# Pooled attention and a two-layer network on one core: transposes by DMA, halved products and new constants in a planner

## The chip, the core and the metric

The kernel runs on one core of one Trainium2 chip. What counts is the device time of one launch in microseconds, the median of a few runs. A core has TensorE (PE, matrix products), VectorE (DVE), ScalarE (ACT, here the exponential and the Gelu), GpSimd (POOL) and SyncE (SP); the last two, and ScalarE once, issue DMAs. TensorE writes its results to PSUM, eight banks of 128 x 512 float32. Each engine works through its own queue in order and waits at an instruction until the semaphores that it names have been raised.

## The reference

Attention with pooled keys, and then a two-layer network on its output:

```python
def _attn_ref(q, kv, w_sr):                  # q (4, 12288, 128), kv (4, 384, 32, 128)
    ...
    kv_pool = kv.reshape(B, H // r, r, W // r, r, C).mean(axis=(2, 4))     # r = 4
    kv_flat = kv_pool.reshape(B, -1, C) @ w_sr                             # 768 keys for each batch
    k = v = kv_flat
    s = scale * (q @ k.transpose(0, 2, 1))
    ...
    return (a @ v)                           # a: the softmax of s

def _moe_ref(x, w_in, w_out):                # x (49152, 128), w_in (128, 2048), w_out (2048, 128)
    h = x @ w_in
    g = h * (1.0 / (1.0 + np.exp(-1.702 * h)))
    return g @ w_out
```

Keys and values are the same numbers, needed in two layouts: keys with the channels on the partitions, values with the key index on the partitions.

## The kernel before

**Tiling.** The 49,152 queries are 96 groups (G = 512). In attention a group has 6 chunks of 128 keys, in the network 16 chunks of 128 hidden units. For every chunk TensorE makes one product of 512 columns into a PSUM bank ("filling": L350 in attention, L596 in the network), ScalarE applies its function to up to three banks in one activation (L352, L598) and writes bf16 to one of 34 frames of three in SBUF, and TensorE multiplies that again ("draining"): in attention 4 products of 129 columns per chunk (L363; the 129th column of the values is one and gives the softmax's sum), in the network one product of 512 columns (L606), accumulated over 16 chunks in one bank. VectorE normalizes the attention output (L386, L389), and turns the network's output bank in blocks of 32 x 32 (L617), from where SP stores it in four DMAs (L619).

**Stages.** Two rounds of 48 groups: attention of groups 0 to 47, their network, attention of 48 to 95, their network. Attention outputs go through DRAM and come back transposed (`put_away`, `bring_back`) as input of the network.

**Banks.** Six of the eight banks are two sets of three which fillings use in turn, so filling p + 2 must wait until activation p has left its set. The other two (four before the activations become three wide) are accumulators, handed out by `acc()`.

**Order.** Everything is placed while the kernel is built, by a planner at the end of the function (L797 to L861). It keeps a model time `now` of TensorE in units of one 512-column product, and `end[p]`, the time at which activation p would end. After each filling it places drains and extras until the next would go past `limit`, the time at which the coming filling must start if its activation is to follow without a gap; then it places that filling. What it has placed stays in that order on the chip, whatever ScalarE really does. The line that says how long an activation is taken to last:

```python
end.append(begin + FIXED + CHUNK * len(part))            # L791; FIXED 0.295, CHUNK 1.978
```

`room_ahead` (free frames) makes it drain when frames run short. At the very end `drain_last` (L622) makes the last group's drains as 64 products of 128 columns in four banks of their own; one of these is the bank of group 94's output ("held"), whose first three products come after the nine of the other banks.

**Offloaded chunks.** A few chunks are computed by VectorE and not by ScalarE: `rolling` and groups 48 to 51 in attention (L415 and `early_exp`), `lent` in the network (L409 and `lent_gelu`). They are 50 of 2112.

**Queries.** Groups 0 to 11 are loaded by POOL's queue with a cast (`load_q`, L222) and transposed on TensorE (`transpose_q`, L236), with a copy by VectorE (L242). From group 12 on POOL casts them to DRAM (`cast_q`, L209) and SP loads them transposed, four groups at a time (`load_qT`, L215), at the groups that TURN names.

**Keys of batches 2 and 3.** They are summed by accumulating DMAs of POOL (`add_kv`, L173), one step for each group of the first network stage from group 2 (batch 2) and 24 (batch 3) on. Then, in two halves a, VectorE adds (`sum_kv`, L179), TensorE transposes the pooled half (L184), and makes keys (`make_k`, L192) and values (`make_v`, L199), each with a copy by VectorE. These three are extras that the planner places between drains.

Of the kernel before, what the change touches and what calls it, by code (L numbers as in the profile page):

```python
# [10 lines left out]
BF = mybir.dt.bfloat16  # L11
# [13 lines left out]
def kernel(  # L25
    ctx, tc, q, kv, w_sr, moe_w_in, moe_w_out, out,
):
    nc = tc.nc
    B, N, C = q.shape
    _, H, W, _ = kv.shape  # L30
    r = 4
# [18 lines left out]
    x_bf = nc.dram_tensor("x_bf", (B * N, C), BF, kind="Internal").ap()  # L50
    q_bf = nc.dram_tensor("q_bf", (B * N, C), BF, kind="Internal").ap()

    kv_r = kv.rearrange("b (ch p) (a w) c -> b a ch p (w c)", p=128, a=2)
# [44 lines left out]
    def acc_bf():  # L98
        return acc().bitcast(BF)
# [20 lines left out]
    def new_keys(b):  # L120
        kTs[b] = kvres.tile([128, J], BF, name="kT")

        vs[b] = kvres.tile([128, JC, C + 8], BF, name="v")
        nc.vector.memset(vs[b][:, :, C:C + 1], 1.0)
# [55 lines left out]

    def transpose_pooled(b, a):
        ps = acc_bf()[:, 0:h].rearrange("p (a b) -> p a b", a=4)
        for wp in range(4):
            nc.tensor.transpose(ps[:, wp, :], pooled[b, a][:, wp, :], ident[:Hp, :Hp])  # L184
        pTs[b, a] = kvtmp.tile([128, h], BF, name="pT")
        nc.vector.tensor_copy(pTs[b, a], ps.rearrange("p a b -> p (a b)"))

    def make_k(b, a):
        ps = acc()
        if a == 0:  # L190
            new_keys(b)
        nc.tensor.matmul(ps[:, :h], w_sr_sb, pTs[b, a], start=True, stop=True)  # L192
        nc.vector.tensor_copy(kTs[b][:, a * h:(a + 1) * h], ps[:, :h])

    def make_v(b, a):
        ps = acc()
        pT = pTs.pop((b, a))
        for k in range(K):
            nc.tensor.matmul(ps[:, k * C:(k + 1) * C], pT[:, k * 128:(k + 1) * 128], w_sr_sb,  # L199
                             start=True, stop=True)  # L200
        nc.vector.tensor_copy(vs[b][:, a * K:(a + 1) * K, 0:C], ps[:, :h].rearrange("p (k c) -> p k c", k=K))
        for jc in range(a * K, a * K + K):
            vs[b, jc] = True
# [13 lines left out]

    QS = 3
    qs = [x_tile(XS - 1 - JC - s) for s in range(QS)]

# [34 lines left out]
    load_q(1, 2, 4)  # L255
    for s in range(2, QS):
        load_q(s, 0, 2)
        load_q(s, 2, 4)
    cast_q(3)
# [70 lines left out]
    early = range(NG // R, NG // R + EARLY)  # L330
    rolling = [(i, JC - 1) for i in [10, *range(38, NG // R, 6), *range(57, 90, 6)]]
    lent = [(g, FCH - 1) for g in range(52, 94) if g % 5 in (2, 4)]
# [189 lines left out]

    TURN = {6: 3, 7: 4, 8: 5, 20: 6, 21: 7, 22: 8, 25: 9, 32: 10, 35: 11, 40: 12}
    CAST = {0: [5], 13: [6], 14: [7], 15: [8], 16: [9], 26: [10, 11], 27: [12]}
# [31 lines left out]
    def background_moe(g):  # L556

        n, g = divmod(g, 4 * XS)
        m, odd = divmod(g - 9, 2)
        m += FIRST  # L560
        if n == 0 and FIRST <= m < RT // PART:
            (bring_back if odd else put_away)(n, m)
        g += n * 4 * XS
        nonlocal low
        if g == 12:
            low = EARLY * JC
            order[:] = [f for f in order if f >= low // K]
        if g in CAST_MOE:
            gate()
            cast_q(CAST_MOE[g])  # L570
        if g in (41, 42):
            load_qT(g - 28)
        if g == 43:
            background(early[0])
        for b, lo in ((2, 2), (3, 24)):
            if lo <= g < lo + 8:
                gate()
                add_kv(b, g - lo)
            if g in (lo + 10, lo + 12):
                use_kv(b, (g - lo - 10) // 2)  # L580

    def use_kv(b, a):
        nonlocal extra_at
        sum_kv(b, a)
        on_dve(3.5)
        extra_at = max(extra_at, dve + 1.5)
        extras.extend([(transpose_pooled, b, a), (make_k, b, a), (make_v, b, a)])

# [10 lines left out]

    def drain_moe(g, fc):  # L600
        if g == NG - 1:
            drain_last(g, fc)
            return
        if fc == 0:
            o_of[g] = acc(("o", g))
        nc.tensor.matmul(o_of[g], w_out_sb[:, fc, :], weights(("m", g, fc)),  # L606
                         start=(fc == 0), stop=(fc == FCH - 1))
        if (g, fc) in lent:
# [102 lines left out]
    def prepare(p):  # L711
# [3 lines left out]
        for i, jc in part:  # L715
# [23 lines left out]
        16: [(key_and_value, 0, 5), (later, 6)],  # L739
        17: [(later, 7)],  # L740
        18: [(later, g) for g in range(8, 12)]}

    FIXED, CHUNK, SWITCH, HANDOVER, EVACUATE = 0.295, 1.978, 6.0, 1.0, 4.5
    COST = {pool_chunk: (1.9, 2.6), key_chunk: (0.3, 2.4), value_chunk: (0.3, 2.4),
            transpose_q: (1.05, 4.2), early_fill: (1.0, 5.5), key_and_value: (0.55, 3.5),
            transpose_pooled: (0.9, 3.6), make_k: (0.8, 3.2), make_v: (0.8, 3.7)}
    COPY = {pool_chunk: 1.5, key_chunk: 1.5, value_chunk: 1.5, key_and_value: 2.8, transpose_q: 3.2}  # L750
# [3 lines left out]
    end, extra_at = [], 0.0  # L754
    source, dve = None, 0.0
    early_left = 2 * (G // T) * EARLY
# [12 lines left out]
    def fill(p):  # L769
# [15 lines left out]
        if p >= 2:  # L785
            now = max(now, end[p - 2] + HANDOVER / 2)
        now += len(part)
        begin = max(now + HANDOVER / 2, end[p - 1] if p else 0.0)
        if p and kind != seq[p - 1][0]:
# [7 lines left out]
    for n in range(len(seq)):  # L797
        fill(n + 2)
        jobs(n + 3)
        while True:  # L800
            room = room_ahead()
            limit = end[-1] - len(seq[n + 3][1]) - HANDOVER if n + 3 < len(seq) else 1e9
            bank = free[next_acc()]
# [10 lines left out]
            if f:  # L814
                now = max(now, bank) + COST[f][0]
                f(*args)
                free[last_acc] = dve + 1.0 if f is early_fill else copied(f)
                if f in (transpose_pooled, make_k, make_v):
                    on_dve(2.5)
                extra_at = max(now + PAUSE, dve + 1.5 if f in (transpose_pooled, make_k, make_v) else 0.0)  # L820
                if f is early_fill:
# [13 lines left out]
            needs = at[("at" if kind == "a" else kind, i, c)]  # L835
            cost = K * SMALL if kind == "a" else 1.0
            halved = kind == "a" and i // TS < SPLIT
            first_of = (c == 0 or halved) and (kind == "m" or i % TS == 0)
            if source is not todo_early and (needs > n or (kind == "a" and first_of and at["at", i + TS - 1, c if halved else 1] > n)
# [5 lines left out]
                break  # L845
            start = now if source is todo_early else max(now, end[needs] + HANDOVER)
            if first_of:
                start = max(start, bank)
            if start + cost > limit and not (room < 2 * K + 1 or (room < 4 * K and start == now)):
                if first_of:  # L850
                    source = None
                break
            now = start + cost
            (drain_attn if kind == "a" else drain_moe)(i, c)
            source.pop(0)
# [37 lines left out]
```

## Time and profile before

| | us |
|---|---|
| runs | 948.50, 948.76, 948.81 (median 948.76) |
| span of the profiled execution | 946.7 |
| Gelu activations of 1536 columns (L598) | 501, 1.496 each as recorded |
| exponentials of 1536 columns (L352) | 161, 1.500 each as recorded |
| first-layer products (L596) | 405.8 busy, 1476 recorded |
| second-layer products (L606) | 402.6 busy, 1477 recorded |
| values' products (L363), 129 columns | 163.0 busy, 2268 recorded |
| query products (L350) | 145.0 busy, 498 recorded |
| query transposes on TensorE (L236) | 4.6 busy, 48 |
| transposes of pooled keys (L184) | 1.3 busy, 16 |
| value products of batches 2 and 3 (L199) | 1.3 busy, 12 |

Times are from the hardware profiler, of one execution. Its span goes from the first to the last instruction; the time of a run is what the device took for the launch, 2.1 us more in the median. Busy time counts each moment once where records overlap, and records of neighbouring products and of neighbouring activations do overlap; so a mean duration is not the pace. The pace is the distance between starts, or between ends. The granted TensorE clock is 1.000 of full speed over the span.

### The profile page before, as it was taken

The numbers are of one execution on the slowest core, as the hardware profiler recorded it, in microseconds if no ns is written. First come the engines' busy times: TensorE is split into PE (matmuls) and PEld (weight loads), VectorE is DVE, ScalarE is ACT, GpSimd is POOL, SyncE is SP. The second block draws the span as 40 slices with busy tenths as digits, with TensorE's granted clock in tenths as the row PEclk, the third lists the DMA queues.
The fourth block names the chain that finished last, engine by engine and source line by source line (L and its number), as shares of the span: only waits on it lengthen the run. The fifth ranks groups of instructions, "written<-read, shape, count | busy, mean of one in ns | idle before, by whom it ended". The sixth has DMA issues, their size and how long they took to land.

```text
span 946.7 us, 15374 instructions
## 1 busy us (share of the span) xinstructions
PE 933.9 (99%) x6200; PEld 502.5 (53%) x6314; DVE 575.1 (61%) x1091; ACT 933.5 (99%) x709; POOL 66.5 (7%) x115
## 2 busy tenths in 40 slices
PE   8999999999999999999999999999999999999998
PEld 4677776444444444444446777744444444444444
DVE  5753653011678776667765765376767766777651
ACT  6999999999999999999999999999999999999998
POOL 3101001330000232000000000000000000000000
PEclk9999999999999999999999999999999999999999
DMA  9997943999867799865335683552222222222222
GB/s 210 195 207 168 181 92 52 130 163 170 164 117 114 119 147 119 127 99 87 56 58 105 138 170 84 119 123 42 36 39 40 38 41 34 44 34 45 34 45 46
DMA packets 372856, 95.46 MB, mean 101 GB/s; under 512 B 346720, under 2 KB 370400, under 8 KB 372320
## 3 DMA queue, kind: packets, MB, share of 16 engines
q1 hardware_dynamic: 344000, 62.36, 36.9%
q0 software_dynamic: 28512, 31.99, 22.3%
q8 instruction: 49, 0.80, 0.3%
q14 instruction: 23, 0.19, 0.1%
q10 hardware_dynamic: 272, 0.13, 0.0%
HBM read 52.49 MB, written 48.76 MB: 107 GB/s over the span
## 4 chain that ended last, share of the span: by engine, by line
PE 97%; ACT 1%; DMA 1%; issue 1%; DVE 0%; POOL 0%; POOLq 0%
PE banks L606 35%; PE banks L596 34%; PE banks L363 14%; PE banks L350 12%; ACT ag L352 1%; PE banks L415 1%; DMA x<-in_kv_dram 1%; PE banks L139 0%; PE banks L409 0%; PE banks L634 0%; PE banks L236 0%; POOL x L222 0%; PE banks L161 0%; PE banks L294 0%; PE banks L192 0%
## 5 line engine op out<-in xcount | busy, mean ns | idle before, releaser
L598 ACT ACTIVATE ag<-banks 128x1536 bf16<-128x1536 f32 (+1 forms) x509 | 681.1, 1489 | 0.0
L596 PE MATMUL banks<-x,w_in_sb 128*128 128x512 bf16 x1476 | 405.8, 379 | 1.7
L606 PE MATMUL banks<-ag,w_out_sb 128*128 128x512 bf16 x1477 | 402.6, 379 | 1.7
L352 ACT ACTIVATE ag<-banks 128x1536 bf16<-128x1536 f32 (+2 forms) x192 | 245.6, 1421 | 3.5 <-PE banks L236 2.3
L606 PEld LDWEIGHTS <-w_out_sb 128*128 128x128 bf16 x1520 | 148.3, 98 | 177.2 <-issue 0.2
L596 PEld LDWEIGHTS <-w_in_sb 128*128 128x128 bf16 x1519 | 147.1, 98 | 171.3 <-issue 0.7
L617 DVE STREAM_TRANSPOSE o_sb<-banks 128x512 f32<-128x512 f32 x95 | 68.1, 717 | 171.4 <-PE banks L606 166.9
L363 PEld LDWEIGHTS <-ag 128*128 128x128 bf16 x2268 | 145.5, 98 | 44.6 <-issue 0.3
L363 PE MATMUL banks<-v,ag 128*128 128x129 bf16 x2268 | 163.0, 220 | 0.2
L350 PE MATMUL banks<-qT,kT 128*128 128x512 bf16 x498 | 145.0, 379 | 3.5 <-ACT ag L352 0.5
L442 DVE SCALAR_TENSOR_TENSOR ea<-ea,eb 128x512 f32<-128x512 f32 x132 | 90.4, 685 | 3.7 <-DVE ea L442 0.7
L386 DVE RECIPROCAL rec<-banks 128x3 f32<-128x3 f32 x124 | 22.3, 180 | 85.3 <-PE banks L363 84.9
L389 DVE TENSOR_TENSOR x<-banks,rec 128x384 bf16<-128x384 f32 x124 | 69.1, 557 | 4.3
L350 PEld LDWEIGHTS <-kT 128*128 128x128 bf16 x543 | 45.8, 98 | 25.9 <-issue 2.0
L473 DVE RECIPROCAL eb<-ea 128x256 f32<-128x256 f32 x34 | 57.6, 1724 | 0.5
L466 DVE SCALAR_TENSOR_TENSOR ea<-ea,eb 128x512 f32<-128x512 f32 x68 | 46.5, 683 | 1.9
L173 POOL DMA_DIRECT2D kvs<-in_kv_dram x32 | 40.4, 1323 | 19.3 <-DMA kvs<-in_kv_dram 17.1
L431 DVE TENSOR_SCALAR ea<-banks 128x512 f32<-128x512 f32 x33 | 22.8, 692 | 29.6 <-PE banks L415 29.2
L521 POOL MEMSET gate_tile<- 1x1 f32 x38 | 3.4, 89 | 325.8 <-DVE gate_tile L520 325.8
L453 DVE TENSOR_SCALAR qT<-banks 128x512 f32<-128x512 f32 x17 | 11.8, 692 | 20.7 <-PE banks L409 20.6
L437 DVE SCALAR_TENSOR_TENSOR eb<-eb,ea 128x512 f32<-128x512 f32 x33 | 22.8, 691 | 0.9
L444 DVE SCALAR_TENSOR_TENSOR ag<-ea,ee 128x512 bf16<-128x512 f32 x24 | 16.6, 691 | 1.2
(83 smaller groups left out, 286.3 us busy)
## 6 DMA issues: line engine op xcount, KB each, us to landing
out_dram<-o_sb SPq DMA_DIRECT2D x380, 64.0 KB, 2.0
kvs<-in_kv_dram POOLq DMA_DIRECT2D x32, 384.0 KB, 6.3
q_bf<-in_q_dram POOLq DMA_DIRECT2D x21, 512.0 KB, 6.6
x_bf<-x SPq DMA_DIRECT2D x13, 768.0 KB, 5.6
x<-in_kv_dram POOLq DMA_DIRECT2D x11, 512.0 KB, 10.4
x_bf<-x SPq DMA_DIRECT2D x6, 384.0 KB, 4.6
x<-in_q_dram POOLq DMA_DIRECT2D x5, 256.0 KB, 15.3
x<-in_kv_dram SPq DMA_DIRECT2D x1, 1024.0 KB, 5.0
```

The costliest lines, as they stand in the source:

```text
L173: nc.gpsimd.dma_start(out=kv_sums[b][:, i2], in_=kv_p[b, i, w, :, i2], **({"accum_op": ADD} if n else {}))
L350: nc.tensor.matmul(ps[:, k, :], kTs[i // GB][:, jc * 128:(jc + 1) * 128], rhs, start=True, stop=True)
L352: nc.scalar.activation(place([("a",) + c for c in chunks]), ps, AF.Exp, scale=scale)
L363: nc.tensor.matmul(av_of[u][:, k * (C + 1):(k + 1) * (C + 1)], weights(("a", i, jc))[:, o:o + T], vs[i // GB][:, jc, 0:C + 1], start=(jc = ...
L389: nc.vector.tensor_tensor(to, ps[:, :, 0:C], rec.unsqueeze(2).broadcast_to([128, TS, C]), MUL)
L442: nc.vector.scalar_tensor_tensor(a, a, COEFFS[k], b, ADD, MUL)
L466: nc.vector.scalar_tensor_tensor(a, a, COEFFS[k], b, ADD, MUL)
L473: nc.vector.reciprocal(b[:, m:m + 256], a[:, m:m + 256])
L596: nc.tensor.matmul(ps[:, k, :], w_in_sb[:, fc * 128:(fc + 1) * 128], x[:, g % (4 * XS) * G:(g % (4 * XS) + 1) * G], start=True, stop=True)
L598: nc.scalar.activation(place([("m",) + c for c in chunks]), ps, AF.Gelu_apprx_sigmoid)
L606: nc.tensor.matmul(o_of[g], w_out_sb[:, fc, :], weights(("m", g, fc)), start=(fc == 0), stop=(fc == FCH - 1))
L617: nc.vector.transpose(o_sb, o_of.pop(g))
```

## The change

1. Groups 8 to 11 are no longer loaded and transposed on TensorE: QS goes from 3 to 2, `cast_q(2)` takes the place of the two loads in POOL's queue, and `load_qT(2)` is issued at group 5.
2. For batches 2 and 3 the pooled half goes to DRAM and comes back transposed, the keys are made from it by a product as before, and the values are the keys, sent to DRAM and loaded transposed. `make_v` and `transpose_pooled` are gone. The steps are two groups apart. Batch 2's sums begin at group 0, not 2. The values' tile has a pitch of C + 16.
3. A second-layer product may be made in two halves of 256 columns, one before and one after the filling that would not wait for the whole.
4. The planner's constants change: FIXED from 0.295 to 0.25; HANDOVER (1.0, used whole or half) becomes RELEASE (0.8 after an exponential, 1.6 after a Gelu) and LATENCY (0.95).
5. Of the offloaded chunks, the one of group 10 moves to group 32.

```diff
-    def transpose_pooled(b, a):
...
+    def put_pooled(b, a):
+        nc.sync.dma_start(out=pool_bf[b, a].rearrange("w h c -> h w c"), in_=pooled[b, a])
+
+    def turn_pooled(b, a):
+        pTs[b, a] = kvtmp.tile([128, 1, h], BF, name="pT")
+        nc.sync.dma_start_transpose(out=pTs[b, a], in_=pool_bf[b, a].rearrange("w h c -> (w h) c"))
+
+    def put_k(b, a):
+        jc = slice(a * K, a * K + K)
+        nc.sync.dma_start(out=k_bf[b, jc].rearrange("j c t -> c j t"),
+                          in_=kTs[b][:, a * h:(a + 1) * h].rearrange("c (j t) -> c j t", t=128))
+
+    def turn_k(b, a):
+        for jc in range(a * K, a * K + K):
+            nc.sync.dma_start_transpose(out=vs[b][:, jc:jc + 1, 0:C], in_=k_bf[b, jc])
...
-    def make_v(b, a):
...
-    QS = 3
+    QS = 2
...
-    for s in range(2, QS):
-        load_q(s, 0, 2)
-        load_q(s, 2, 4)
+    cast_q(2)
     cast_q(3)
...
-    rolling = [(i, JC - 1) for i in [10, *range(38, NG // R, 6), *range(57, 90, 6)]]
+    rolling = [(i, JC - 1) for i in [*range(32, NG // R, 6), *range(57, 90, 6)]]
...
-    TURN = {6: 3, 7: 4, 8: 5, 20: 6, 21: 7, 22: 8, 25: 9, 32: 10, 35: 11, 40: 12}
+    TURN = {5: 2, 6: 3, 7: 4, 8: 5, 20: 6, 21: 7, 22: 8, 25: 9, 32: 10, 35: 11, 40: 12}
...
-        for b, lo in ((2, 2), (3, 24)):
+        for b, lo in ((2, 0), (3, 24)):
...
+            for a in range(2):
+                step = g - lo - 9 - a
+                if step == 0:
+                    sum_kv(b, a)
+                    on_dve(3.5)
+                    put_pooled(b, a)
+                if step == 2:
+                    turn_pooled(b, a)
+                if step == 4:
+                    extras.append((make_k, b, a))
+                if step == 6:
+                    put_k(b, a)
+                if step == 8:
+                    turn_k(b, a)
...
-        nc.tensor.matmul(o_of[g], w_out_sb[:, fc, :], weights(("m", g, fc)),
-                         start=(fc == 0), stop=(fc == FCH - 1))
+        nc.tensor.matmul(o_of[g][:, lo:hi], w_out_sb[:, fc, :], weights(("m", g, fc))[:, lo:hi],
+                         start=(fc == 0), stop=(fc == FCH - 1 and hi == G))
+        if hi < G:
+            return
...
-    FIXED, CHUNK, SWITCH, HANDOVER, EVACUATE = 0.295, 1.978, 6.0, 1.0, 4.5
+    FIXED, CHUNK, SWITCH, EVACUATE = 0.25, 1.978, 6.0, 4.5
+    RELEASE, LATENCY, HALF = {"a": 0.8, "m": 1.6}, 0.95, 0.506
...
         if p >= 2:
-            now = max(now, end[p - 2] + HANDOVER / 2)
+            now = max(now, end[p - 2] + RELEASE[seq[p - 2][0]])
         now += len(part)
-        begin = max(now + HANDOVER / 2, end[p - 1] if p else 0.0)
+        begin = max(now + LATENCY, end[p - 1] if p else 0.0)
...
-            limit = end[-1] - len(seq[n + 3][1]) - HANDOVER if n + 3 < len(seq) else 1e9
+            limit = end[-1] - len(seq[n + 3][1]) - LATENCY if n + 3 < len(seq) else 1e9
...
+            if kind == "m" and c and not begun_half and i < NG - 1 and start + cost > limit >= start + HALF:
+                drain_moe(i, c, 0, G // 2)
+                now = start + HALF
+                begun_half = True
+                continue
...
+            if begun_half:
+                drain_moe(i, c, G // 2, G)
+                begun_half = False
+            else:
+                (drain_attn if kind == "a" else drain_moe)(i, c)
```

## The prediction

> **What bounds the kernel now.** I read the page first, then the groups with shapes kept apart, then ScalarE's and TensorE's own order of time in each stage, and the end of the span last. The page leaves two candidates:
>
> ```profile
> PE 933.9 (99%) x6200; PEld 502.5 (53%) x6314; DVE 575.1 (61%) x1091; ACT 933.5 (99%) x709; POOL 66.5 (7%) x115
> ```
>
> Busy time can't separate them: TensorE and ScalarE are both at 99%, and the records of both overlap (501 Gelu activations of 1.496 us would fill 749 us; their group says 673.6). So I ask at what pace each one goes, and which of the two keeps its pace while the other's changes.
>
> ```profile
> L598 ACT ACTIVATE ag<-banks 128x1536 bf16<-128x1536 f32 x501 | 673.6, 1496 | 0.0
> L352 ACT ACTIVATE ag<-banks 128x1536 bf16<-128x1536 f32 x161 | 217.1, 1500 | 0.0
> ```
>
> The last column is idle time before the activations: none, in 662 of them. TensorE over a few periods of the second layer stage (start, length of the merged piece, line, count):
>
> ```profile
> 748.06 0.81 PE L596 MATMUL banks<-x,w_in_sb 128*128 128x512 bf16 x3
> 748.70 0.81 PE L606 MATMUL banks<-ag,w_out_sb 128*128 128x512 bf16 x3
> 749.35 0.81 PE L596 MATMUL banks<-x,w_in_sb 128*128 128x512 bf16 x3
> 750.00 0.81 PE L606 MATMUL banks<-ag,w_out_sb 128*128 128x512 bf16 x3
> 750.65 0.81 PE L596 MATMUL banks<-x,w_in_sb 128*128 128x512 bf16 x3
> 751.29 1.03 PE L606 MATMUL banks<-ag,w_out_sb 128*128 128x512 bf16 x4
> ```
>
> From 748.06 to 750.65 are 12 products in 2.59 us: 0.216 us each, back to back. A period with six products takes 1.296 us, one with seven 1.512. ScalarE doesn't follow this alternation:
>
> ```profile
> 39.92 1.45 ACT L352 ACTIVATE ag<-banks 128x1536 bf16<-128x1536 f32 x1
> 45.26 1.48 ACT L352 ACTIVATE ag<-banks 128x1536 bf16<-128x1536 f32 x1
> 50.59 1.53 ACT L352 ACTIVATE ag<-banks 128x1536 bf16<-128x1536 f32 x1
> 53.26 1.55 ACT L352 ACTIVATE ag<-banks 128x1536 bf16<-128x1536 f32 x1
> ...
> 199.12 61.99 ACT L598 ACTIVATE ag<-banks 128x1536 bf16<-128x1536 f32 x46
> 419.45 62.01 ACT L598 ACTIVATE ag<-banks 128x1536 bf16<-128x1536 f32 x46
> 859.19 56.61 ACT L598 ACTIVATE ag<-banks 128x1536 bf16<-128x1536 f32 x42
> ```
>
> The last three are runs without a gap. Less the last member's 1.49 us, they give 60.50/45, 60.52/45 and 55.12/41: 1.344 us each time. The four single ones, members 1, 5, 9 and 11 of one run, are the important ones. They start 1.335 us apart on average, but each lasts longer than the one before, so they end at 41.37, 46.74, 52.12 and 54.81: 1.343, 1.345 and 1.345 us apart. An activation that starts early only lasts longer; ScalarE delivers one per 1.344 us. In that stretch TensorE brought its products (L350) every 1.33 us, so it wasn't TensorE that set the 1.344. I take 1.344 us as ScalarE's own pace for three chunks. Before the change TensorE's average period happens to equal it (below), so both are full; ScalarE's work is what can't shrink.
>
> At the end, TensorE has little left behind its last first-layer pair:
>
> ```profile
> 940.35 0.59 PE L596 MATMUL banks<-x,w_in_sb 128*128 128x512 bf16 x2
> 940.78 2.62 PE L634 MATMUL banks<-w_out_sb,ag 128*128 128x128 bf16 x44
> ```
>
> 44 small products take (2.62 - 0.22)/43 = 0.0558 us each (0.22 is the tail of the last). They end 2 x 0.216 + 44 x 0.0558 = 2.89 us after 940.35, and the span ends 3.4 us later, at 946.7.
>
> **The change, part by part.** The counts are from the instruction order of the two kernels, the durations from the rows.
>
> *Removed from TensorE:* 16 transposes for query groups 8 to 11 (0.9 us at 0.0558), 16 of pooled keys (at most 0.9 by the same row, since they are narrower) and 12 value products (0.67): 2.2 to 2.5 us. VectorE loses four query copies of 0.69, four of 0.36 and four of 0.56 us.
>
> *Halves:* 240 second-layer products become 480 of 256 columns. No row shows 256 columns. From 129 columns (twelve in 0.68 us between two starts at L363, 0.0566 each) and 512 (0.216) a straight line gives 0.1094, so a pair costs 0.003 us more than the whole one: 0.7 us. Bounds: nothing (half of 0.216), and 2.5 us (a half as dear as two of the 129-column ones). I take 0.7, so TensorE's work falls by about 1.6 us.
>
> None of this reaches the end if ScalarE is what is full. Its work is the same: 2 single, 37 double and 662 triple activations in both orders.
>
> *The planner.* This is the part that costs. It counts in products. Its activation of three chunks was 0.295 + 3 x 1.978 = 6.229 products, at 0.216 us 1.3455 us: what ScalarE does. It becomes 0.25 + 5.934 = 6.184, or 1.336 us: faster than ScalarE is. The order is fixed when the kernel is built, so TensorE gets about 0.01 us too little second-layer work per period, then waits in its queue for ScalarE to free a bank, with the unfinished products behind the wait. The orders show it. In 200 periods of the last stage, 630 second-layer products become 620 (halves counted as half); with 600 first-layer ones and 15 for VectorE's chunks TensorE's mean period goes from 1245 x 0.216/200 = 1.345 us to 1.334; from the first to the last first-layer product of that stage, 752 become 730. After the last first-layer pair, 44 small products become 22 whole and 64 small ones. That is 0.43 + 22 x 0.216 + 64 x 0.0558 = 8.75 us instead of 2.89, and ScalarE has nothing left to do under it: **+5.87 us** on the end.
>
> A further wait is in that tail. The last group's small products use the bank of group 94 from their tenth on. VectorE must first turn that bank: before, the last two products of group 94 began at 937.90 and ended at 938.33, the turn began at 938.53 and takes 0.72, so it is done 0.92 to 0.97 us after the products. Nine small products cover 0.50: **+0.45 us** (before, two first-layer products stood between; bounds 0 and 0.7).
>
> *What ScalarE gains.* With TensorE less loaded its own waits can go. In the first attention stage its 73 steps from 41.27 to 139.91 are 1.351 us each, 0.5 us over pace. At the start, 29 doubles take 27.65 us from 12.27, 0.953 each against 0.906 in a run of nine from 30.68: up to 1.4 us, much of it behind key copies that stay. The Gelu stages spread from 1.343 to 1.346: 0.6 at most over 500. Together 0 to 2.5 us; I take **-1.1**.
>
> *Queries 8 to 11 by DMA.* Two loads become one cast of the same bytes in POOL's queue and a transposing load in SP's, which must wait for the cast.
>
> ```profile
> 11.33 0.70 POOL L222 DMA_DIRECT2D x<-in_q_dram  x1 [0.54 <-DMA x<-in_q_dram]
> ...
> DMA to landing us min/median/max: 15.3/15.3/15.3
> ...
> DMA to landing us min/median/max: 4.2/5.7/7.0
> ```
>
> The second replaced load is issued at 11.33 and lands 15.3 later, at 26.6; the three transposing loads of that time take 4.2 to 7.0 us (the longest of all 21, 8.3). So qT of groups 8 to 11 is there between 30.8 and 34.9, most likely near 33.6 like the first one (7.0). Group 8's first pair, the 26th fill, is at 33.60 in TensorE's order of time. Cover is nil at worst: loss 0 to 1.3 us, and everything behind that fill on TensorE would stand. I take **+0.3**. The loads of groups 12 on queue behind it in SP; 12's first fill is some 10 us later.
>
> *Pooled keys and values by DMA.* 24 more DMAs on SP (4 stores and 4 loads of pooled, 4 of keys, 12 of values), POOL's sums of batch 2 two groups earlier. Each step stands two groups (some 14 us) behind the last, longer than the longest landing of the 21 transposing loads; the output stores they stand among have three buffers, and values are first used a stage later. Cost nothing; without that cover a late value would hold ScalarE one for one. The chunk that moves from group 10 to 32 on VectorE is free as well (61% busy).
>
> Two rules of the Trainium skill were weighed here. "ScalarE: Activation LUTs", section "What ACT_TABLE_LOAD costs", gives 186 ns + 0.833 ns per element less an overlap of 93 ns, 1.373 us for 1536 columns; the runs above show 1.344, and 662 times the difference (19 us) wouldn't fit into the span, so the rows decide. The sum is the same by either, for the tail is counted in products. "DMA: Bandwidth & Descriptors", section "Rules for kernel authors", speaks against the change: transfers under 64 KB pay mostly overhead, and each value block is 32 KB. The nearest row, 64 KB stores, lands in 2.0 us; by rule or row it ends within the two groups, and the sum stays.
>
> **Sum.** 946.7 + 5.87 + 0.45 - 1.1 + 0.3 = 952.2 us of span. The median shown is 948.76, 2.1 over the profiled span, which lies around it: **954.3 us**, 0.6% slower.
>
> **Rivals.** *TensorE is the bound (not slower).* If ScalarE can really go at the 1.335 us at which its activations start, nothing piles up: TensorE's 1.6 us come off, 947.1 us; with 0.6 of waits at the start, 946.5. For it: TensorE is 99% busy and the chain of waits is 97% TensorE. Against it: the ends at 1.344, and runs of 1.344 whatever TensorE brought. It decides where ScalarE's period is under TensorE's new one, 1.336. Chance 0.07.
>
> *Queries late.* If the transposing load starts later or lands slower than any shown, by 3 us beyond 33.6, 957 us. For it: no spare cover, and the first such load was slow. Against it: SP's queue is empty then. Chance 0.08.
>
> *SP's queue.* Three value blocks in one group at 1.6 to 2.0 us of issue each plus four stores at about 0.5 make 6.8 to 8 us against a group's 7.2; only if that repeats do stores fall behind three buffers and the banks with them: a few us more, 958. Chance 0.03.
>
> The forecast itself has 0.82. Its bounds: 948.8 + 5.87 - 2.5 = 952.2 and 948.8 + 5.87 + 0.7 + 1.3 = 956.7; I cut the upper end to 956.4. A measurement of this kernel can tell about 0.2% (1.9 us) from no change: the first rival lies on the edge, so faster and same get 0.04 each with a little for waits that I missed, and slower 0.92.
>
> **What would show it.** Right: in the new profile ScalarE's runs still go at 1.344, TensorE has small idle times before first-layer products released by ScalarE, and ScalarE ends some 7 us before TensorE's last product, with 22 whole and 64 small products behind the last first-layer pair. Wrong: ScalarE's runs at 1.336 or less with TensorE back to back, or a gap of ScalarE near 34 us.

## The result, and the profile after

| | before | after |
|---|---|---|
| median of the runs, us | 948.78 (948.50 to 948.89, 4 runs) | 958.34 (958.19 to 958.45, 4 runs) |
| ratio | | 1.0101 [1.0087, 1.0116] |
| span of the profiled execution, us | 946.7 | 956.4 |

The change makes the kernel 1.0% slower. The forecast was 954.3 us with a range of 952.2 to 956.4: the direction is right, the time lies outside the range.

The page of the kernel after, with its engines, its chain of waits and its largest group:

```profile
PE 946.7 (99%) x6510; PEld 524.8 (55%) x6510; DVE 569.2 (60%) x1080; ACT 932.7 (98%) x709; POOL 65.4 (7%) x114
...
ACT 52%; PE 45%; DMA 2%; issue 0%; DVE 0%; POOL 0%; SPq 0%; POOLq 0%
...
L604 ACT ACTIVATE ag<-banks 128x1536 bf16<-128x1536 f32 (+1 forms) x509 | 680.6, 1702 | 0.0
```

ScalarE has as much work as before (932.7 us busy against 933.5), and TensorE's time is still 99% covered by its records. What changed is the chain that ended last: now more than half of it is ScalarE, and before it was 97% TensorE:

```profile
PE 97%; ACT 1%; DMA 1%; issue 1%; DVE 0%; POOL 0%; POOLq 0%
```

The mean recorded duration of a Gelu activation of 1536 columns rose from 1.496 to 1.711 us (the 1.702 of the line above has eight shorter ones among them) while no idle time stands before them, so it says only that activations overlap more, not that they are slower. Their pace shows in ScalarE's order of time, in the three runs without a gap (start, length, line, count):

```profile
198.58 62.18 ACT L604 ACTIVATE ag<-banks 128x1536 bf16<-128x1536 f32 x46
...
418.90 62.17 ACT L604 ACTIVATE ag<-banks 128x1536 bf16<-128x1536 f32 x46
...
698.45 62.18 ACT L604 ACTIVATE ag<-banks 128x1536 bf16<-128x1536 f32 x46
```

Less the 1.70 us of the last member, 60.48/45 = 1.344 us: the pace of before, to three digits.

The end of the span on TensorE, which before had only 44 small products behind its last first-layer pair:

```profile
943.50 0.59 PE L602 MATMUL banks<-x,w_in_sb 128*128 128x512 bf16 x2
943.93 4.91 PE L612 MATMUL banks<-ag,w_out_sb 128*128 128x512 bf16 x22
948.67 0.67 PE L642 MATMUL banks<-w_out_sb,ag 128*128 128x128 bf16 x9
949.65 3.23 PE L642 MATMUL banks<-w_out_sb,ag 128*128 128x128 bf16 x55 [0.30 <-DVE o_sb L625]
```

22 whole and 64 small products are left behind the pair, and between the ninth and the tenth small one TensorE waits for VectorE's turn of the held bank (the bracket: idle time and what ended it). From the start of the pair to the end of the span are 12.9 us; before, 946.7 - 940.35 = 6.35. ScalarE's last activation ends at 945.28, 7.6 us before TensorE's last product (952.88), as the prediction had asked for.

That accounts for 6.55 of the 9.7 us. The other 3.15 must lie ahead of the pair, which starts at 943.50 and not at 940.35. ScalarE's groups with their idle time, in the view of the waits (what waited, for what; us in total, times, longest):

```profile
ACT ag L353 <- PE banks L351: 7.0, 5, 2.8
...
PE banks L351 <- DMA qT<-q_bf: 2.8, 1, 2.8
```

In before the same view has 3.0 us of such waits, in two lines:

```profile
ACT ag L352 <- PE banks L236: 2.3, 1, 2.3
...
ACT ag L352 <- PE banks L350: 0.7, 1, 0.7
```

So some 4 us are new. The second line of after is a wait that before didn't have: query products of TensorE wait for a transposing load. Where it is, in ScalarE's order of time:

```profile
29.58 4.72 ACT L353 ACTIVATE ag<-banks 128x1024 bf16<-128x1024 f32 x5
37.13 1.02 ACT L353 ACTIVATE ag<-banks 128x1024 bf16<-128x1024 f32 x1 [2.83 <-PE banks L351]
38.45 1.02 ACT L353 ACTIVATE ag<-banks 128x1024 bf16<-128x1024 f32 x1 [0.29 <-PE banks L351]
40.28 8.16 ACT L353 ACTIVATE ag<-banks 128x1024 bf16<-128x1024 f32 x7 [0.81 <-PE banks L351]
```

One idle time of 2.83 us near 34 us, the place that the prediction had named as the one that would show it wrong, and two smaller ones behind it which no load explains. TensorE at that time, and then stretch by stretch (busy time and count of PE, PEld, DVE, ACT and POOL, then the granted clock, DMA share, GB/s):

```profile
33.00 0.67 PE L364 MATMUL banks<-v,ag 128*128 128x129 bf16 x9
36.49 0.60 PE L351 MATMUL banks<-qT,kT 128*128 128x512 bf16 x2 [2.81 <-DMA qT<-q_bf]
...
37.35 1.06 PE L351 MATMUL banks<-qT,kT 128*128 128x512 bf16 x2
```

```profile
36.00:37.00 1.00, 0.51 (x4) 0.28 (x5) 0.00 (x0) 0.00 (x0) 0.00 (x0) 1.00 1.15 218
37.00:38.00 1.00, 1.00 (x9) 0.65 (x8) 0.00 (x0) 0.87 (x1) 0.00 (x0) 0.58 1.06 239
38.00:39.00 1.00, 1.00 (x9) 0.79 (x8) 0.00 (x0) 0.70 (x2) 0.00 (x0) 0.50 1.13 188
39.00:40.00 1.00, 1.00 (x6) 0.49 (x5) 0.74 (x2) 0.47 (x1) 0.00 (x0) 0.50 1.29 231
40.00:41.00 1.00, 1.00 (x11) 0.88 (x10) 0.00 (x0) 0.72 (x1) 0.00 (x0) 0.71 1.11 177
```

TensorE stands for 2.81 us, starts again at 36.49, and some 0.7 us later its granted clock falls to 0.50 (a mean of 0.58 from 37 to 38 is full speed until 37.16), where it stays until about 40.6 (0.71 in the last stretch): a pair of query products then takes 1.06 us as recorded instead of 0.60, and TensorE can't keep ScalarE fed. So two causes had to be told apart: how much the planner's constant costs, and how much the late queries cost, with the clock as a part of it.

### The profile page after: what moved, and what is told of

Same layout as the page of the kernel before. It is cut to its first block, busy times and chain, and to the rows that moved or that the text cites. A ratio compares the mean times of both kernels' runs of the same rounds, so it can differ in the third digit from the quotient of the medians.

```text
span 956.4 us, 15896 instructions
## 1 busy us (share of the span) xinstructions
PE 946.7 (99%) x6510; PEld 524.8 (55%) x6510; DVE 569.2 (60%) x1080; ACT 932.7 (98%) x709; POOL 65.4 (7%) x114
## 3 DMA queue, kind: packets, MB, share of 16 engines
q1 hardware_dynamic: 352864, 64.46, 36.2%
## 4 chain that ended last, share of the span: by engine, by line
ACT 52%; PE 45%; DMA 2%; issue 0%; DVE 0%; POOL 0%; SPq 0%; POOLq 0%
ACT ag L604 36%; PE banks L602 17%; PE banks L612 17%; ACT ag L353 16%; PE banks L364 5%; PE banks L351 5%; DMA qT<-q_bf 1%; DMA x<-in_kv_dram 1%; PE banks L410 0%; PE banks L642 0%; PE banks L141 0%; DMA out_dram<-o_sb 0%; DVE o_sb L625 0%; ACT L353 0%; ACT L604 0%
## 5 line engine op out<-in xcount | busy, mean ns | idle before, releaser
L602 PE MATMUL banks<-x,w_in_sb 128*128 128x512 bf16 x1519 | 410.4, 378 | 0.0
L612 PE MATMUL banks<-ag,w_out_sb 128*128 128x512 bf16 (+1 forms) x1741 | 407.0, 350 | 0.0
L612 PEld LDWEIGHTS <-w_out_sb 128*128 128x128 bf16 x1760 | 171.7, 98 | 181.7 <-issue 0.2
L364 PE MATMUL banks<-v,ag 128*128 128x129 bf16 x2268 | 165.1, 221 | 0.0
L351 PE MATMUL banks<-qT,kT 128*128 128x512 bf16 x543 | 149.3, 380 | 4.3 <-DMA qT<-q_bf 2.8
L351 PEld LDWEIGHTS <-kT 128*128 128x128 bf16 x543 | 46.7, 98 | 29.1 <-DMA qT<-q_bf 3.0
L454 DVE TENSOR_SCALAR qT<-banks 128x512 f32<-128x512 f32 x17 | 11.8, 691 | 36.4 <-PE banks L410 36.4
```

What stands on the lines that cost most here:

```text
L351: nc.tensor.matmul(ps[:, k, :], kTs[i // GB][:, jc * 128:(jc + 1) * 128], rhs, start=True, stop=True)
L364: nc.tensor.matmul(av_of[u][:, k * (C + 1):(k + 1) * (C + 1)], weights(("a", i, jc))[:, o:o + T], vs[i // GB][:, jc, 0:C + 1], start=(jc = ...
L602: nc.tensor.matmul(ps[:, k, :], w_in_sb[:, fc * 128:(fc + 1) * 128], x[:, g % (4 * XS) * G:(g % (4 * XS) + 1) * G], start=True, stop=True)
L612: nc.tensor.matmul(o_of[g][:, lo:hi], w_out_sb[:, fc, :], weights(("m", g, fc))[:, lo:hi], start=(fc == 0), stop=(fc == FCH - 1 and hi == G))
```

## The experiments

All ratios are against the kernel before, run on the same chip in the same rounds (its medians there: 948.43 for the first four, 948.54 for the next four, 948.55 for the last two).

**1. Queries 8 to 11 back on TensorE.**

```diff
-    QS = 2
+    QS = 3
...
-    cast_q(2)
+    for s in range(2, QS):
+        load_q(s, 0, 2)
+        load_q(s, 2, 4)
...
-    TURN = {5: 2, 6: 3, 7: 4, 8: 5, ...
+    TURN = {6: 3, 7: 4, 8: 5, ...
...
+        18: [(later, g) for g in range(8, 12)]}
```

> The changed kernel with one part undone: queries of groups 8 to 11 are loaded and transposed on TensorE again, all else as changed. Theory A (the late transposing load and the halved TensorE clock behind it cost 4.5 us at 34 to 45 us of the span, and the rest of the loss is the tail behind ScalarE's end): no gap of ScalarE near 34 us, and a tail counted from this kernel's own order, 32 whole and 64 small products behind the last first-layer pair: 0.43 + 32 x 0.216 + 64 x 0.0558 = 10.9 us against 2.9 before, +8.0, +0.45 for the held bank, -1.3 of ScalarE's waits: 948.8 + 7.2 = 956.0 us. Rival B (the extra 4 us over the forecast come from ScalarE or TensorE being slower all along the span): the gap goes but the time stays 4 us over this sum, 960 us.

Measured 955.91 us (955.60 to 955.99), 1.0077 [1.0062, 1.0092]. The idle time near 34 us and the fall of the clock are gone (granted 1.00 from 33 to 39). That is only 2.4 us better than after, but the order isn't the same at the end. TensorE's last rows before the small products:

```profile
939.08 0.59 PE L604 MATMUL banks<-x,w_in_sb 128*128 128x512 bf16 x2
939.51 7.07 PE L614 MATMUL banks<-ag,w_out_sb 128*128 128x512 bf16 x31
```

The last first-layer pair starts at 939.08, 4.42 us earlier than in after. Behind it are 31 whole products and not 22, and its tail lasts 954.0 - 939.08 = 14.92 us instead of 12.90. So the late queries cost 4.4 us, of which this order gives 2.0 back in the tail. Against before the pair starts 1.27 us earlier (940.35): that is what ScalarE gains from a TensorE with less between its fillings (experiments 3 and 4 show which part of the change does that).

**2. Only the planner's FIXED back at 0.295.**

```diff
-    FIXED, CHUNK, SWITCH, EVACUATE = 0.25, 1.978, 6.0, 4.5
+    FIXED, CHUNK, SWITCH, EVACUATE = 0.295, 1.978, 6.0, 4.5
```

> The changed kernel with the planner's FIXED put back from 0.25 to 0.295. Theory A (the wrong activation time in the planner makes the tail): 44 small products are left behind the last first-layer pair, as before the change, so the tail's 5.9 us and the held bank's 0.45 go; the late queries stay: 958.3 - 6.3 = 952.0 us, ScalarE's gap of 3 us at 34 us as it was. Rival B (the tail is TensorE's work that would come anyway, TensorE being the bound): no more than 1 us better, 957.3 or more.

Measured 952.37 us (952.01 to 954.92, 4 runs), 1.0046 [1.0031, 1.0061]. The tail is the one of before, 44 small products:

```profile
944.14 0.59 PE L602 MATMUL banks<-x,w_in_sb 128*128 128x512 bf16 x2
944.57 2.62 PE L642 MATMUL banks<-w_out_sb,ag 128*128 128x128 bf16 x44
```

The pair starts 0.64 us later than in after, and nothing whole is left behind it. The wait at 34 us and the clock at 0.50 are still there. The constant alone thus costs 958.34 - 952.37 = 6.0 us, or 5.6 with each of the two taken against before on its own chip (9.56 less 3.94).

**3. Both back** (the edits of 1 and 2 together; the pooled keys by DMA, the halves, RELEASE and LATENCY stay).

> Both of the two others together: queries 8 to 11 on TensorE, FIXED 0.295; halves, the new waits of the planner and the pooled keys by DMA stay. Theory A: no gap at 34 us; the order leaves 64 small products behind the last first-layer pair, 0.43 + 3.57 = 4.0 us against 2.9, +1.1; ScalarE's small waits gone, -1.3: 948.8 - 0.2 = 948.6 us. Rival B (something else in the change costs, such as halves or 24 more DMAs): 950 us or more.

Measured 948.92 us (948.68 to 949.99, 10 runs), 1.0005 [0.9996, 1.0015]. Everything else in the change, taken together, is worth nothing that can be measured. The two causes together explain the whole of the loss. The last first-layer pair starts at 940.11 here, only 0.24 us earlier than in before, although TensorE has been relieved of the same work as in after but for the queries.

**4. The kernel before with FIXED 0.25**, its only edit.

```diff
-    FIXED, CHUNK, SWITCH, HANDOVER, EVACUATE = 0.295, 1.978, 6.0, 1.0, 4.5
+    FIXED, CHUNK, SWITCH, HANDOVER, EVACUATE = 0.25, 1.978, 6.0, 1.0, 4.5
```

> The kernel before with one number changed, FIXED from 0.295 to 0.25. Theory A (ScalarE takes 1.344 us for three chunks whatever the planner thinks): the order leaves 32 whole and 64 small products behind the last first-layer pair, 10.9 us against 2.9: +8.0, +0.45 for the held bank, -1.0 of ScalarE's waits: 956.2 us. Rival B (ScalarE can go at 1.335 us, TensorE is the bound): 948.8 us or a little less, with TensorE still back to back.

Measured 955.73 us (955.69 to 955.77), 1.0076 [1.0061, 1.0091]. TensorE's order of time at the end:

```profile
939.46 7.07 PE L606 MATMUL banks<-ag,w_out_sb 128*128 128x512 bf16 x31
```

The same 31 whole products as in 1, now without a DMA or a half of the change. The last first-layer pair starts at 939.03, 1.32 us earlier than in before. A constant in a model of time, which changes no instruction but their order, makes 0.8%.

**5. The casts of the later queries moved away from the first transposing load.** If the load is late because POOL's casts run then, it should be early without them.

```diff
-    cast_q(3)
-    cast_q(4)
...
-    TURN = {5: 2, 6: 3, 7: 4, 8: 5, ...
-    CAST = {0: [5], ...
+    TURN = {5: 2, 8: 3, 9: 4, 10: 5, ...
+    CAST = {7: [3], 8: [4], 9: [5], ...
```

(with FIXED 0.295)

> The changed kernel with FIXED 0.295 and the casts of groups 12 to 23 moved from the start to groups 7, 8 and 9 (their transposing loads to groups 8, 9 and 10); queries 8 to 11 stay on DMA. Theory A (the transposing load of groups 8 to 11 stands behind the casts issued after its own: in both traces no byte of it moves before these have ended at about 32 us): alone, it moves at once when its own cast has landed at 26.5 and lands 4 to 5 us later, by 31.5, before 33.6; no gap of ScalarE at 34 us, TensorE's clock stays at 1.0: 948.4 + 0 (44 small products behind the last pair, as before) - 1.0 of ScalarE's waits = 947.4 us. Rival B (the first transposing load is slow by itself, 7 to 10 us whatever runs beside it): it lands at 34 to 36 as before, 950 to 952 us.

Measured 1003.59 us (994.94 to 1021.28), 1.0539 [1.0507, 1.0571]: a miss of 56 us, and the most telling run. The first load did what was expected: issued at 26.9, it landed 4.4 us later instead of 9.7, and the idle time at 34 us is gone. But the next two loads, issued at 39.4 and 44.4 us, met six loads of keys that POOL issues at 40.4 and 44.4, and landed only after 34.1 and 39.9 us. The waits of this kernel, and three of its stretches:

```profile
ACT ag L351 <- PE banks L349: 59.5, 7, 29.8
...
PE banks L349 <- DMA qT<-q_bf: 53.5, 2, 29.1
```

```profile
45.00:50.00 5.00, 0.00 (x0) 0.00 (x0) 0.00 (x0) 0.22 (x1) 1.01 (x2) 0.95 1.37 35
50.00:60.00 10.00, 0.00 (x0) 0.00 (x0) 0.00 (x0) 0.00 (x0) 0.00 (x0) 0.50 1.26 62
60.00:70.00 10.00, 0.00 (x0) 0.00 (x0) 0.00 (x0) 0.00 (x0) 0.00 (x0) 0.50 1.02 142
```

From 50 to 60 us no engine works; the 16 DMA engines count as more than full (1.26), yet only 62 GB/s move. A transposing load and POOL's large loads that meet both crawl: the six key loads land after 27.9 to 36.1 us here, where the median of the key loads in after is 9.7. A third transposing load, issued at 78.8 us when POOL issues casts again, takes 42.2 us, but nothing waits for it.

**6. TensorE kept busy while it waits.** Is the fall of the clock a matter of the wait, or of something that comes with the DMAs? 14 products whose results nobody reads stand ahead of group 8's first pair, in the after kernel. They are computed on top of the reference's work.

```diff
+    def keep_busy(n):
+        ps = acc()
+        for _ in range(n):
+            nc.tensor.matmul(ps[:32, :], ones, ones.unsqueeze(1).broadcast_to([128, 16, 32]),
+                             start=True, stop=True)
...
+        25: [(keep_busy, 14)]}
```

> The changed kernel with 14 products of 512 columns, whose result nobody reads, put in front of group 8's first pair, where TensorE stands for 2.8 us. Theory A (the clock falls to half because TensorE stood still): the wait for the load stays, the clock stays at 1.0, and ScalarE's three later gaps of 0.40, 0.91 and 0.25 us go: 958.3 - 1.5 = 956.8 us. Rival B (the clock falls for another reason): the three gaps stay, 958.3 us or, where the 14 products outlast the wait, up to 0.5 more.

Measured 957.00 us (956.87 to 957.07), 1.0089 [1.0076, 1.0102]. TensorE's order of time, then its stretches:

```profile
33.17 3.19 PE L138 MATMUL banks<-ones 128*32 128x512 bf16 x14
...
36.82 0.59 PE L357 MATMUL banks<-qT,kT 128*128 128x512 bf16 x2
...
37.59 0.59 PE L357 MATMUL banks<-qT,kT 128*128 128x512 bf16 x2
```

```profile
37.00:38.00 1.00, 1.00 (x10) 0.63 (x9) 0.47 (x2) 0.55 (x1) 0.00 (x0) 1.00 1.13 253
38.00:39.00 1.00, 1.00 (x13) 0.74 (x12) 0.40 (x2) 1.00 (x2) 0.00 (x0) 1.00 1.15 177
```

The load comes as late as in after (issued at 27.07, landed 9.4 us later), but the clock stays at 1.00, the pairs take 0.59 us, and the smaller idle times behind the first are gone. The tail is that of after, 22 whole and 64 small products, and its pair starts 1.27 us earlier (942.23 against 943.50), although the unread products hold group 8's pair up for 0.33 us more. The time falls by 958.34 - 957.00 = 1.3 us (1.1 with each taken against before on its own chip). So 1.1 to 1.3 us of the 4.4 were the clock; some 3 are the wait itself.

**7. Pooled keys and values of batches 2 and 3 back on TensorE**, on top of 3 (`transpose_pooled`, `make_v` and batch 2's later start as in before).

```diff
-        for b, lo in ((2, 0), (3, 24)):
+        for b, lo in ((2, 2), (3, 24)):
...
+        extras.extend([(transpose_pooled, b, a), (make_k, b, a), (make_v, b, a)])
```

> Queries 8 to 11 on TensorE, FIXED 0.295, and pooled keys and values of batches 2 and 3 on TensorE as before the change; halves and the planner's other constants stay. Theory A (the transposes by DMA are free, and so are the products that they save, since ScalarE is full): 64 small products behind the last pair as in the run with queries and FIXED put back, so the same time, 948.9 us within 0.5. Rival B (24 DMAs more on SP cost something): 1 us or more faster than that run. Rival C (TensorE's work still counts): 1.3 us slower.

Measured 949.22 us (949.05 to 950.88, 10 runs), 1.0012 [1.0004, 1.0021]; number 3 has 948.92. What TensorE is spared there doesn't reach the end. Four of the ten runs took 950.65 to 950.88; what set them apart was not followed.

**8. No halves**, on top of 3.

```diff
-            if kind == "m" and c and not begun_half and i < NG - 1 and start + cost > limit >= start + HALF:
+            if False and kind == "m" and c and not begun_half and i < NG - 1 and start + cost > limit >= start + HALF:
```

> Queries 8 to 11 on TensorE, FIXED 0.295, and no product split into halves; the planner's new waits stay. Theory A (time is ScalarE's end plus what the order leaves behind it): the order leaves 70 whole and 64 small products behind the last first-layer pair: 0.43 + 70 x 0.216 + 64 x 0.0558 = 19.1 us against 4.0 with halves, +15.1, and the held bank's 0.45: 948.9 + 15.5 = 964.4 us; TensorE idle, released by ScalarE. Rival B (what is not split is only moved, and TensorE catches up): 950 us.

Measured 967.04 us (966.97 to 967.08), 1.0194 [1.0180, 1.0209]. Behind the last first-layer pair (942.27) are now 37 + 1 + 32 whole products:

```profile
942.70 8.15 PE L614 MATMUL banks<-ag,w_out_sb 128*128 128x512 bf16 x37
...
950.90 7.07 PE L614 MATMUL banks<-ag,w_out_sb 128*128 128x512 bf16 x32
```

With the new LATENCY and RELEASE a whole product fits less often before a filling, so TensorE is filled less (its first-layer weight loads stand idle for 67.3 us, 397 times, against 0.3 us once in number 3) and more is left for the end: 18 us. The halves are what makes the change's own limits bearable. The time is 2.6 us above what was expected, and the pair starts 2.2 us later than in 3 (940.11). Of that, 1.0 is ScalarE's waits for first-layer products (1.2 us in this run, 0.2 in number 3), the rest was not followed. That frames ran short there is possible, and no run shows it.

**9. Late queries mended: the casts in between.** Casts 3 to 5 go into one step at group 6, the transposing loads follow at groups 7 to 9, and batch 1's key loads come two groups later, so that no load of SP's should meet one of POOL's; FIXED is 0.295.

```diff
-    TURN = {5: 2, 6: 3, 7: 4, 8: 5, ...
-    CAST = {0: [5], ...
+    TURN = {5: 2, 7: 3, 8: 4, 9: 5, ...
+    CAST = {6: [3, 4, 5], ...
...
-        if i in (10, 12):
+        if i in (12, 14):
```

> The changed kernel with FIXED 0.295, queries 8 to 11 still by DMA, and POOL's transfers moved so that none runs beside SP's transposing loads of the start: the casts of groups 12 to 23 at group 6, their transposing loads at groups 7, 8 and 9, batch 1's key loads at groups 12 and 14 (were 10 and 12), their pooling two groups later. Theory A (a transposing load that meets transfers of POOL stands or crawls until they end, and lands in 4 to 5 us alone): no gap of ScalarE at 34 us nor later, 28 small products behind the last first-layer pair, 2.0 us against 2.9, and 1.0 of ScalarE's waits gone: 948.5 - 0.9 - 1.0 = 946.6 us. Rival B (the loads of groups 12 to 23 still meet transfers): a gap of 3 us or more between 44 and 80 us, 950 us or more.

Of 12 runs seven took 948.07 to 948.82 us and five 958.9 to 971.5; the ratio, taken over the nine shortest, is 1.0024 [0.9995, 1.0052]. The median of the seven is 948.22, against 948.55 in before and 946.6 as expected. The execution that was profiled took 948.13. In it the first load landed after 5.3 us and no engine waits for a transposing load of queries, and still it is no better than before. Its end on TensorE:

```profile
940.47 0.94 PE L640 MATMUL banks<-w_out_sb,ag 128*128 128x128 bf16 x14
941.87 0.95 PE L640 MATMUL banks<-w_out_sb,ag 128*128 128x128 bf16 x14 [0.46 <-ACT ag L602]
```

The last 14 products wait for ScalarE's last activation. From the last first-layer pair (940.03) to the end are 6.37 us, as many as the 6.35 of before, with 28 small products there and not 44. TensorE is ahead, ScalarE is the end: fewer products on TensorE gain nothing there. Why five executions took 10 to 23 us more wasn't profiled; a transfer that meets another, as in number 5, would look like that, and no run shows it.

**10. The other side of the constant: FIXED 0.31** with the queries on TensorE.

```diff
-    FIXED, CHUNK, SWITCH, EVACUATE = 0.25, 1.978, 6.0, 4.5
+    FIXED, CHUNK, SWITCH, EVACUATE = 0.31, 1.978, 6.0, 4.5
```

> Queries 8 to 11 on TensorE and FIXED 0.31, a little over what ScalarE does. Theory A (the tail follows the planner's count, and ScalarE stays full as long as the planner isn't far over its pace): 28 small products behind the last first-layer pair, 2.0 us against 4.0 with 0.295, and 0.015 products per activation (2 ns by 662) of ScalarE's waits more at most, 1.3 us, rather 0.5: 948.9 - 2.0 + 0.5 = 947.4 us. Rival B (over its pace the planner makes ScalarE wait for all of it): 948.2 us or more.

Measured 949.47 us (949.35 to 949.80, 11 runs), 1.0010 [1.0001, 1.0019]. The tail has the 28 small products, but the time is that of rival B, 2.1 us over what was expected. Here too TensorE's last 14 products wait 0.46 us for ScalarE, which ends 1.6 us later than in number 3 (943.51 against 941.89). Its 662 triple activations cover 891.9 us, against 890.2 in number 3, and no idle time shows before them: its pace has become slower. That it waits for first-layer products which the planner placed later is the likely reason, since only the constant differs. A model slower than ScalarE holds ScalarE back; one that is faster leaves work for the end. Between 0.295 and 0.31 they nearly balance (948.92 and 949.47), and no version beats before by more than can be measured.

## Why the prediction was right in its direction and wrong in its size

**ScalarE is what is full, at 1.344 us.** Right. The pace is the same in after and, with the constant lowered alone (experiment 4), ScalarE didn't go at 1.336: work piled up behind its end instead. Experiments 9 and 10 show the floor itself: TensorE idles at the very end, for ScalarE. The rival that TensorE is the bound falls: it asked for 947 us. (The starts that it went by are 1.334 us apart, 13.34 us over ten steps, and not 1.335; nothing hangs on that.)

**The planner's constant: +5.87 for the tail, +0.45 for the bank.** Right. The tail took 12.90 us against 6.35, 6.55 more, where the two terms make 6.32. The bank's turn made TensorE stand for 0.30 us after the ninth product's recorded end; from 948.67 nine products of 0.0558 us end at 949.18, and the tenth starts at 949.65, 0.47 later. Experiment 2 measures the whole of the constant by undoing it, 5.6 to 6.0 us, and experiment 4 by doing it alone in the kernel before, 7.3 us (955.73 - 948.43, there with 31 whole products left and not 22). The waits that were to show it are too short to be seen one by one; they appear in the view of the waits as idle time of first-layer weight loads, for which the profile knows no releaser:

```profile
PEld L602 <- issue: 9.9, 59, 0.3
```

From 600 to 940 us it is 4.8 us in 28 of them, against 0.2 in one before. They follow the constant: over the span 0.7 us in before and 9.9 with FIXED alone changed (experiment 4), 9.9 in after and 0.5 with FIXED alone put back (experiment 2). That they are waits for banks which ScalarE holds is inferred from this; the view names no releaser.

**ScalarE's waits gone: -1.1.** Right in size: 1.27 by the start of the last first-layer pair in experiment 1 (939.08 against 940.35). It comes from the constant, and hardly from the work taken off TensorE: with FIXED alone lowered (experiment 4) the pair is 1.32 us earlier than in before, with FIXED at 0.295 and TensorE relieved in part (experiment 3) or wholly (experiment 9) 0.24 and 0.32 us. In before the planner's 1.3455 us was itself a little over ScalarE's 1.344, and 662 times the difference is 1.0 us. So the loss at the end and this gain are two sides of one number.

**Halves, and work removed from TensorE.** Right that they don't reach the end, and 256 columns take 0.11 us between two starts (938.59 and 938.70 in experiment 1; forecast 0.1094). That the halves are needed was not said: without them the new limits cost 18 us (experiment 8).

**Pooled keys and values by DMA: nothing.** Right (experiments 3 and 7). So the rival "SP's queue", whose 958 us lies nearest to the measured time, is not what happened.

**Queries 8 to 11 by DMA: +0.3, bounds 0 to 1.3.** This is the step that failed, in its size and in its upper bound. It cost 4.4 us. The prediction took the load's landing as issue plus 4.2 to 8.3 us, as other transposing loads show it; with an issue at 26.6 that is 30.8 to 34.9. It was issued as forecast, at 26.73, but took 9.7 us and landed at 36.4. What happened in between is in the DMA view of after, for the stretch from 26.8 to 31.5 us, with the load issued (queue and kind, packets, MB, share of the 16 engines):

```profile
q0 software_dynamic: 64, 1.05, 104.5%
q8 instruction: 1, 0.02, 1.2%
q1 hardware_dynamic: 3, 0.00, 0.1%
```

POOL's queue is q0, and SP's loads are on q1. For almost five microseconds the transposing load moved 3 packets; from 32 to 37 us q1 moved 3391, of this load and the next. What ran before it were POOL's casts of the next queries, issued at 11.4, 12.7 and 15.2 us, which landed at 29.1, 32.2 and 34.1: the load's bytes begin to move about when they come to their end. Experiment 5 is the test: with all three of these casts moved to later groups, the same load lands after 4.4 us. Whether the load stands in line behind the casts or only shares the DMA engines with them, of which q0 alone takes 104.5% in that stretch, stays open. The 7.0 us of the first such load in before, which the prediction took as a slow landing, was the same thing. Its trace had it, in the DMA view from 29.3 to 32 us, when that load had been issued at 29.22:

```profile
q0 software_dynamic: 32, 0.52, 91.1%
q8 instruction: 1, 0.02, 2.3%
```

There is no line for q1 at all. A load issued 2.5 us earlier behind much the same casts has nothing to gain from it; with the landing of 36.2 that before shows (29.22 + 7.0), the wait at 33.6 would have been put at 2.6 us; it measured 2.8. The rival "Queries late" had this size (3 us, 957) and a chance of 0.08; it came on top of the forecast, and it was held back by "SP's queue is empty then", which was true and didn't matter, since what held the load was the other queue's transfers. The remaining 1.1 to 1.3 us, TensorE's clock after its wait, were in no step: the prediction priced a wait of TensorE at its own length.

**The sum, with what was measured:** 946.7 - 1.27 + 4.42 + 6.55 = 956.4 us of span. It closes by construction, since the 4.42 and the 1.27 are both taken from the pair of experiment 1; what bears it out is experiment 3, in which both causes are gone and 948.92 us remain.

## What to carry to other kernels

A constant that tells a static order how long an engine takes must come from its deliveries, from end to end over a long run: starts and durations overlap, and a model 0.6% too fast (1.336 for 1.344 us) moved 6 us of work behind the end, and one 0.4% too slow (FIXED 0.31, 1.349 us) slowed ScalarE by 1.7 us (experiment 10 against 3). A load that is moved earlier is bounded from when its bytes can move, which the DMA view by queue shows, and not from its issue; look for what the other queues carry in that stretch. Where one engine is full almost from the first to the last microsecond, every wait of it costs its length, a wait of the engine that feeds it can cost more than its length by the clock that follows, and taking work off that other engine brought nothing here.

## What the runs showed of the hardware that was not expected

- A transposing load on SP's queue stands while POOL's casts and large loads run: 4.4 us from issue to landing alone, 9.7 beside the end of three casts (after), 34.1 and 39.9 beside six key loads, with 62 GB/s moved by all queues together for 10 us (experiment 5). The price is not one of the transfer but of its neighbours. The Trainium skill, "DMA: Bandwidth & Descriptors", section "Rules for kernel authors", says that transfers under 64 KB pay mostly overhead. This case fits it, as far as a transposing load and a plain store can be compared: in after the 32-KB value loads land in 2.4 us, the 64-KB stores in 1.9.
- TensorE's granted clock falls to 0.50 after a wait of 2.8 us, some 0.7 us after work has begun again and 3.5 us after the last product before it, and stays there for about 3.4 us (after). That work begins again is not what lowers it: in experiment 5 it falls at about 49.5 us, in the middle of a wait, 5.2 us after TensorE's last product (44.36). Without the wait, with products that nobody reads, it stays at 1.00 (experiment 6), which is worth 1.1 to 1.3 us.
- Queued activations started 1.334 us apart in the attention stage of before while they delivered one per 1.344. After the change the mean recorded duration of a Gelu activation is 1.711 us, 0.215 more than before, and the delivery still 1.344: the duration depends on how early an activation may start, and the pace doesn't.
